# Re-timing one batch's input loads around a second-stage group, and two warm-up products, in a Fourier-mixing and feed-forward kernel

## The chip, the core and the metric

The kernel runs on one core of a Trainium2 chip. The metric is device time in microseconds (us) from the start to the end of one execution. Unless marked otherwise, times inside the kernel are counted in us from the first instruction of the profiled execution.

The engines have short names in the profile: PE is TensorE (matrix products, with PEld its weight loads), DVE is VectorE, ACT is ScalarE, POOL is GpSimd, and SP is SyncE, which here only issues transfers (DMAs).

## What is computed

```python
def _attn_ref(x):                       # x: (8, 3008, 256) float32
    X = np.fft.fft(x, axis=1)
    X = np.fft.fft(X, axis=2)
    return X.real.astype(np.float32)

def _moe_ref(x, w_in, w_out):           # x: (24064, 256), w_in: (256, 2048), w_out: (2048, 256)
    h = x @ w_in
    g = h * (1.0 / (1.0 + np.exp(-1.702 * h)))
    return (g @ w_out).astype(np.float32)
```

The output is `_moe_ref` of the first function's result, its eight batches laid end to end.

## The kernel before

**Work and steps.** The Fourier transform along the 3008 rows is split as 47 x 64. For each batch there is a first stage (`mix1`, products with the tables `w1`), a turn through a DRAM buffer (`spill` writes it, `fill` reads it back in three parts of 512 KB), a small rotation of one column (`rotate`), and a second stage (`stage2`, three groups of 64 small products). The transform along the 256 columns is folded into `w_in` at the start (`fold_w`), so that the feed-forward part reads the second stage's result directly. The main loop has 48 steps for a batch, 384 in all; a step takes one pair of 128-row blocks of the hidden layer for half of a second-stage group. In a step t, `begin` forms the hidden products, `forward` (line 649) is the activation on ACT, `sums` on POOL and DVE and `deeper` on DVE prepare operands of a fast matrix product, and `product` and `small_products` of step t - 3 and t - 4 form the output. Eight steps make a group, whose result is turned by DVE (line 793) and stored by four DMAs for each half; the halves go out near the end of the next eight steps (in batch 0, for instance, in steps 38 and 39, and 46 and 47).

**Work put between.** What belongs to the next batches is hung on steps with `at(t, fn, ...)` (line 987). A table `PLANS` (line 984) holds, for a batch b, the steps within it for: the 16 folds of batch b + 1 on POOL (`fold1`, lines 245 to 251, two parts for each of 8 chunks), the four first-stage groups of batch b + 1 (`mix1`), the first of the three fills (`filled`), the rotation, the four loads of batch b + 2 into the tile `xt` (`load_x`, line 212), and the three second-stage groups. Batch 0 has a row of its own, all others share the second row. A fold step can be negative: those folds of batch b + 1 then run in the last steps of batch b - 1.

So the x of batch 2 is loaded in steps of batch 0, and its first four folds run at steps 46 to 49: two at the end of batch 0, two at the start of batch 1. A fold reads all 111 partitions of `xt`, and so waits for all four loads. Each load is two DMAs, one from x and one from a mirrored copy `Xr`: 512 KB each for loads 0 and 2, 240 KB each for loads 1 and 3. The second-stage group of step 44 is that of batch 1's first block.

**Queues.** Nearly all DMAs are issued by SP, in program order: a DMA that waits holds all behind it. `paced(t)` (line 424) is a 4-byte DMA that reads a value that `forward(t)` writes; it holds SP's queue until that activation. Each fill, each load and each turn (`turn`, line 201, which makes `Xr`) has one ahead of it.

**Warm-ups.** `warm(n)` (line 359) does n products of 128 columns by 512 whose result nobody reads, each as two matmul instructions. In the start, before the main loop, two stand beside `fold_w(0)`: one before it and one (of the tile `small`) after it. `stage2(0, 0)` (line 979) follows, then DVE's transposes of its result (`turn_seconds`, line 400), which the first hidden products (`hidden`, tiles pa and pb) wait for.

Of the kernel before, what the change touches and what calls it, by code (L numbers as in the profile page):

```python
# [51 lines left out]
def free(ap, offset, *dims):  # L52
    return bass.AP(ap.tensor, ap.offset + offset, [list(ap.ap[0])] + [list(d) for d in dims])
# [68 lines left out]
def kernel(ctx: ExitStack, tc, x, w_in, w_out, tab1, tab2, out):  # L122
# [25 lines left out]
    small = const.tile([128, 4 * NB + 128 + 4 * H], F32, tag="small", name="small")  # L148
# [30 lines left out]
    def bank(name, tag=None):  # L179
        if tag is None:  # L180
            tag = spare.pop(0)
            spare.append(tag)
        if tag in ("o0", "o1"):
            return o_banks[int(tag[1])]
        if tag[0] == "l":
            return pot["low"][:, 512 * int(tag[1]):512 * int(tag[1]) + 512]
        return (rest if tag[0] == "o" else psp).tile([128, 512], F32, tag=tag, name=name)
# [171 lines left out]
    def warm(n, tag=None, of=wcs[0]):  # L359

        ps = bank("warm", tag)
        for _ in range(n):
            nc.tensor.matmul(ps[:], lhsT=of[:, 0:128], rhs=of[:, 0:512], start=True, stop=True)
# [11 lines left out]
    def rotate(b, a0=0, a1=NG, copy=None):  # L375

        col = t4t[b][:, a0:a1, H]
        ps = bank("psr")
        halves(ps[:, 0:a1 - a0], rot, col, start=True, stop=True)
        (copy or nc.vector.tensor_copy)(col, ps[:, 0:a1 - a0])  # L380

    def stage2(b, blk):

        pq, t4 = pqp.tile([128, 2, 512], F32, tag="pq", name="pq"), t4t[b]
        pqt[b, blk] = pq
        m = m2 if b else m2f
        ps = [bank("ps2") for _ in range(NU)]
        for cs in range(2):
            for h in range(2):
                for g in range(4):  # L390
                    for u in range(NU):
                        rows, at = slice(64 * u, 64 * u + 64), cs * 256 + h * 128
                        nc.tensor.matmul(ps[u][32 * g:32 * g + 32, at:at + 128], lhsT=m[rows, cs, h * RUN:(h + 1) * RUN],  # L393
                                         rhs=free(t4[rows, 4 * blk, cs * H + g // 2 + NB * (g % 2):], 0, [D, 4], [2, 32]),
                                         start=(cs == h == 0), stop=True, skip_group_check=True)
        turning.append((pq, ps, 1 if b or blk else 2))
# [3 lines left out]
    def turn_seconds():  # L400
        for pq, ps, parts in turning:
            for cs, u in [(cs, u) for cs in range(parts) for u in range(NU)]:
                nc.vector.transpose(free(pq[:], cs * 512 + u * RUN, [256, 4 // parts], [NU * RUN, 4], [1, RUN]),
                                    free(ps[u][:], cs * 256, [128, 4 // parts], [32, 4], [1, 32]))
        turning.clear()
# [29 lines left out]
    def load_out(n, eng):  # L435
        t = raw["out", n] = ring("raw").bitcast(U32).rearrange("p (n w) -> p n w", w=2)
        eng.dma_start(out=t[:].rearrange("p (f n) w -> p f (n w)", f=4),
                      in_=w_out[4 * n * 128:(4 * n + 4) * 128, :].bitcast(U32).rearrange("(p f) n -> p f n", p=128))
# [70 lines left out]
    def halved(n):  # L509

        s = summed[n] = pre["in", n][0]
        nc.vector.tensor_tensor(s[:, 0:512], wst[n][:, 0], wst[n][:, 1], op=ALU.add)
        nc.vector.tensor_tensor(s[:, 512:], wst[n][:, 0], wst[n][:, 1], op=ALU.subtract)
# [13 lines left out]
    def fold_w(n, tags=(None, None)):  # L527
        ps = [bank("psw", tag) for tag in tags]
        for cs in range(2):
            if n in summed:  # L530
                for odd_d in range(2):
                    c0 = NB * odd_d
                    nc.tensor.matmul(ps[cs][c0:c0 + NB], lhsT=cd[:, 0, cs, c0:c0 + NB], rhs=summed[n][:, 512 * odd_d:512 * odd_d + 512],  # L533
                                     start=True, stop=True, skip_group_check=True)
        for i in range(2 if n not in summed else 0):
            for cs in range(2):
                halves(ps[cs][:], cd[:, i, cs, :], wst[n][:, i, :], start=(i == 0), stop=(i == 1))
        for cs in range(2):

            nc.scalar.copy(wcs[cs][:, n * 512:(n + 1) * 512].rearrange("p (f c) -> p f c", f=4),  # L540
                           free(ps[cs][:], 0, [1, 4], [4, 128]))
# [428 lines left out]
    for h0 in (0, 512):  # L970
        high(in1, h0, 512)
        finish_in(1, h0, 512)
    load_out(1, nc.sync)
    warm(1, "o0")
    fold_w(0)
    warm(1, "o0", small)
    first_row(0)
    rotate(0, 0, 4, nc.scalar.copy)
    stage2(0, 0)
    turn_seconds()  # L980
    halved(1)

    extra = {}
    PLANS = (((*range(9, 18), 22, 23, 24, 25, 26, 29, 30), (20, 28, 28, 36), 37, 43, (39, 40, 41, 42), (8, 20, 44)),
             ([g + k for g in (0, 8, 16, 24) for k in range(-2, 2)], (4, 20, 28, 28), 31, 35, (36, 38, 40, 42), (4, 20, 36)))

    def at(t, fn, *args):
        extra.setdefault(t, []).append((fn, args))
# [21 lines left out]
    for b in range(B):  # L1010
        t0 = b * NBLK * NF
        if b + 2 < B:
            for k in range(3):
                at(t0 + 11 + k, paced, t0 + 11 + k)
                at(t0 + 11 + k, turn, b + 2, k)
        folds, groups, filled, turned_at, loads, seconds = PLANS[min(b, 1)]
        if b + 1 < B:
            for c in range(NCH):
                for part in range(2):
                    at(t0 + folds[2 * c + part], fold1, b + 1, c, part, nc.gpsimd)  # L1020
                if c % 2:
                    k = t0 + groups[c // 2]
                    at(k, mix1, b + 1, c // 2)
                    for half in range(2):
                            at(k + 1 + (k != 36) * (c // 2 % 2), spill, b + 1, half, c // 2)
            for blk in range(NBLK):
                at(t0 + filled + blk, paced, t0 + filled + blk)
                at(t0 + filled + blk, fill, b + 1, 4 * blk, 4 * blk + 4)
            if b + 2 < B:
                for k in range(4):  # L1030
                    at(t0 + loads[k], paced, t0 + loads[k])
                    at(t0 + loads[k], load_x, b + 2, k)
                at(t0 + 34, paced, t0 + 34)
                at(t0 + 34, load_ends, b + 2)
                at(t0 + 41, fold_ends, b + 2, nc.gpsimd)
            at(t0 + turned_at, rotate, b + 1, 0, NG, nc.scalar.copy)
        for blk in range(NBLK):
            nxt = (b, blk + 1) if blk + 1 < NBLK else (b + 1, 0)
            if nxt[0] < B:
                k = t0 + seconds[blk]  # L1040
                at(k, stage2, *nxt)
                at(k + 1, nyquist_out, *nxt)
                at(k + 1 + (nxt != (1, 0)), nyquist, *nxt)
# [125 lines left out]
```

## Time and profile before

| what | value |
|---|---|
| median of 3 runs | 1838.15 us (1837.58, 1838.15, 1840.1) |
| the profiled execution | 1839.32 us |
| its span, first to last instruction | 1837.5 us |
| mean granted TensorE clock | 0.998 |
| instructions | 55863 |
| DMA queue q1 (SP's) | 148270 packets, 99.09 MB |

One execution is profiled; its rows give durations and idle times of single instructions, its own time is 1.8 us longer than its span. A line of a group reads: line of the code, engine, operation, tile written <- tiles read, shape, count, then busy us and mean ns. A line of a timeline reads: start, duration, engine, line, operation, tiles, shape, count, and in brackets the engine's idle time just before and what ended it; "issue" there means that nothing which the profile shows was waited for. The share of a DMA stretch is the mean over the core's 16 DMA engines and can come out slightly over 1.

### The profile page before, as it was taken

What the parts mean: (1) busy time and instruction counts of PE and PEld (TensorE: products, weight loads), DVE (VectorE), ACT (ScalarE), POOL (GpSimd) and SP (SyncE); (2) the same over time, 40 slices, a digit from 0 to 9 for tenths busy, and PEclk for the clock granted to TensorE, in tenths of its full rate; (3) what the DMA queues carried; (4) which work ended last, traced back from release to release, by engine and by line L of the source; (5) the groups of instructions that cost most, each with busy time, mean ns of one, the idle gap of its engine ahead of it and who ended that gap; (6) DMA issues with size and microseconds to landing.
All of it is one profiled execution on the core that took longest, in us unless ns stands there. A gap on an engine that the chain in (4) does not pass through costs nothing.

```text
span 1837.5 us, 55863 instructions
## 1 busy us (share of the span) xinstructions
PE 1821.4 (99%) x23656; PEld 1400.3 (76%) x23656; DVE 1478.0 (80%) x1927; ACT 1138.0 (62%) x2238; POOL 992.7 (54%) x1070
## 2 busy tenths in 40 slices
PE   8999999999999999999999999999999999999998
PEld 4677777777777777877778777787777877777775
DVE  6988878887888778887888878888788887878774
ACT  4666656665666666666666666666666666656663
POOL 3785446654656546565456644576446653444442
PEclk9999999999999999999999999999999999999999
DMA  8811251113311151212402124021331012100011
GB/s 273 194 53 35 60 99 28 47 35 96 60 45 30 49 115 27 61 27 72 92 22 59 32 67 86 22 64 26 84 69 38 15 26 65 29 21 14 18 24 24
DMA packets 151687, 105.68 MB, mean 58 GB/s; under 512 B 106212, under 2 KB 133094, under 8 KB 150878
## 3 DMA queue, kind: packets, MB, share of 16 engines
q1 hardware_dynamic: 148270, 99.09, 22.3%
q8 instruction: 186, 3.05, 0.7%
q10 hardware_dynamic: 3168, 3.03, 0.6%
q14 instruction: 63, 0.52, 0.1%
HBM read 64.81 MB, written 48.05 MB: 61 GB/s over the span
## 4 chain that ended last, share of the span: by engine, by line
PE 96%; DMA 2%; DVE 1%; issue 0%; POOL 0%; ACT 0%; SPq 0%; DVEq 0%; POOLq 0%
PE x L196 35%; PE o L196 28%; PE low L740 26%; PE o L740 4%; PE low L273 1%; PE low L393 1%; DMA xt<-in_x_dram 1%; PE po L196 0%; DMA Td<-big 0%; DMA big<-in_moe_w_in_dram 0%; DMA Tf<-big 0%; DMA Td<-e 0%; PE psw L533 0%; PE ps L393 0%; POOL xt L905 0%
## 5 line engine op out<-in xcount | busy, mean ns | idle before, releaser
L664 POOL TENSOR_TENSOR big<-big 128x256 f32<-128x256 f32 (+1 forms) x376 | 365.7, 973 | 786.0 <-ACT big L656 772.0
L196 PE MATMUL x<-pq,wcs 128*64 128x256 f32 (+1 forms) x6016 | 765.0, 375 | 0.0
L196 PE MATMUL o<-big,wo 128*64 128x256 f32 (+1 forms) x4800 | 631.1, 376 | 0.0
L196 PEld LDWEIGHTS x<-pq,wcs 128*64 128x64 f32 x6016 | 422.8, 137 | 173.5 <-issue 1.5
L196 PEld LDWEIGHTS o<-big,wo 128*64 128x64 f32 x4800 | 337.7, 137 | 145.3 <-issue 8.2
L646 ACT ACTIVATE g<-x 128x512 f32<-128x512 f32 (+1 forms) x376 | 221.7, 590 | 362.3 <-PE x L196 359.9
L665 POOL TENSOR_TENSOR big<-big 128x256 f32<-128x256 f32 (+1 forms) x376 | 380.0, 1011 | 0.0
L740 PE MATMUL low<-big 128*64 128x128 f32 (+1 forms) x5888 | 377.5, 270 | 0.0
L649 ACT ACTIVATE big<-x 128x512 f32<-128x512 f32 (+1 forms) x376 | 221.7, 590 | 241.0 <-PE x L196 215.3
L634 ACT ACTIVATE x<-nb,af 128x256 f32<-128x256 f32 (+1 forms) x752 | 352.7, 469 | 12.2
L653 DVE TENSOR_TENSOR big<-g,x 128x512 f32<-128x512 f32 (+1 forms) x376 | 250.5, 666 | 132.2 <-ACT big L649 131.5
L740 PEld LDWEIGHTS low<-big 128*64 128x64 f32 x5888 | 335.1, 137 | 25.2
L695 DVE TENSOR_TENSOR big<-big 128x1024 f32<-128x1024 f32 (+1 forms) x184 | 225.4, 1225 | 101.4 <-PE low L740 85.8
L656 ACT ACTIVATE big<-big 128x512 f32<-128x512 f32 (+1 forms) x376 | 231.6, 616 | 24.5 <-DVE big L653 23.4
L740 PE MATMUL low<-big,wo 128*64 128x128 f32 (+1 forms) x2944 | 220.0, 270 | 0.0
L699 DVE TENSOR_TENSOR big<-big 128x512 f32<-128x512 f32 (+1 forms) x184 | 192.0, 1043 | 0.0
L697 DVE TENSOR_TENSOR big<-big 128x512 f32<-128x512 f32 (+1 forms) x184 | 168.1, 914 | 16.6 <-PE o L196 0.9
L740 PEld LDWEIGHTS low<-big,wo 128*64 128x64 f32 x2944 | 172.6, 137 | 6.3
L672 DVE TENSOR_TENSOR big<-big 128x512 f32<-128x512 f32 (+1 forms) x188 | 159.0, 845 | 6.5
L842 DVE TENSOR_TENSOR big<-big,low 128x512 f32<-128x512 f32 (+3 forms) x184 | 109.1, 610 | 35.6 <-PE low L740 32.2
L671 DVE TENSOR_TENSOR big<-big 128x512 f32<-128x512 f32 (+1 forms) x188 | 131.5, 700 | 0.9 <-POOL big L664 0.9
L740 PE MATMUL o<-big,wo 128*64 128x128 f32 (+1 forms) x1472 | 110.0, 270 | 0.0
(119 smaller groups left out, 1124.9 us busy)
## 6 DMA issues: line engine op xcount, KB each, us to landing
out_dram<-os SPq DMA_DIRECT2D x284, 64.0 KB
Td<-xt SPq DMA_DIRECT2D x56, 192.0 KB
t<-Td SPq DMA_DIRECT2D x21, 512.0 KB
xt<-in_x_dram SPq DMA_DIRECT2D x14, 512.0 KB
xt<-Xr SPq DMA_DIRECT2D x14, 512.0 KB
nb<-Nd SPq DMA_DIRECT2D x22, 256.0 KB
out_dram<-os SPq DMA_DIRECT2D x96, 56.0 KB
Xr<-in_x_dram SPq DMA_DIRECT2D x7, 752.0 KB
```

Of the source, the lines that this page charges most:

```text
L196: nc.tensor.matmul(out[c0:c0 + 64], lhsT=lhs[:, c0:c0 + 64], rhs=rhs, skip_group_check=True, **how)
L634: nc.scalar.activation(x[:, i * 256:i * 256 + n], nbt[b, blk][:, hh * 256:hh * 256 + n], ACTF.Copy, scale=af1[:, f:f + 1])
L646: nc.scalar.activation(two(g[:], n), two(xb[t][:], n), ACTF.Copy, scale=2.0)
L649: nc.scalar.activation(front(t), two(xb[t][:], width(t)), ACTF.Gelu_apprx_sigmoid)
L653: nc.vector.tensor_tensor(back(t), two(gt.pop(t)[:], n), two(xb.pop(t)[:], n), op=ALU.subtract)
L656: nc.scalar.activation(back(t), back(t), ACTF.Gelu_apprx_sigmoid)
L664: eng.tensor_tensor(right(t, S1, n), left(t, A21, n), right(t, A22, n), op=ALU.add)
L665: eng.tensor_tensor(left(t, S3, n), left(t, A11, n), left(t, A21, n), op=ALU.subtract)
L695: nc.vector.tensor_tensor(free(big[:], SUM, *both_), free(big[:], from11 + w, *twice), free(big[:], from11, [at_right(t, 0) + w - from11, ...
L697: nc.vector.tensor_tensor(s2, a11, s1, op=ALU.subtract)
L699: nc.vector.tensor_tensor(s4, a12, s2, op=ALU.subtract)
L740: nc.tensor.matmul(o, lhsT=lhs, rhs=rhs, start=first_in, stop=(p == NP - 2), skip_group_check=True)
```

## The change

Four things change in the schedule; no function does.

- In batch 0's plan the three fills of batch 1 move from steps 37, 38, 39 to 38, 39, 40, and the four loads of batch 2 from steps 39, 40, 41, 42 to 41, 42, 45, 46, that is two on each side of the second-stage group of step 44. Each moves with its pacing DMA.
- Batch 1 gets a plan row of its own, in which the first four folds of batch 2 run at steps 47 to 50 in place of 46 to 49. The other twelve stay, and so do the plans of batches 2 and later.
- Ahead of `fold_w(0)` there are two warm-up products in place of one.
- One more warm-up product, of `small`, stands between `stage2(0, 0)` and `turn_seconds()`.

```diff
     load_out(1, nc.sync)
-    warm(1, "o0")
+    warm(2, "o0")
     fold_w(0)
     warm(1, "o0", small)
     first_row(0)
     rotate(0, 0, 4, nc.scalar.copy)
     stage2(0, 0)
+    warm(1, "o0", small)
     turn_seconds()
     halved(1)
...
-    PLANS = (((*range(9, 18), 22, 23, 24, 25, 26, 29, 30), (20, 28, 28, 36), 37, 43, (39, 40, 41, 42), (8, 20, 44)),
+    PLANS = (((*range(9, 18), 22, 23, 24, 25, 26, 29, 30), (20, 28, 28, 36), 38, 43, (41, 42, 45, 46), (8, 20, 44)),
+             ([g + k for g in (1, 8, 16, 24) for k in range(-2, 2)], (4, 20, 28, 28), 31, 35, (36, 38, 40, 42), (4, 20, 36)),
              ([g + k for g in (0, 8, 16, 24) for k in range(-2, 2)], (4, 20, 28, 28), 31, 35, (36, 38, 40, 42), (4, 20, 36)))
...
-        folds, groups, filled, turned_at, loads, seconds = PLANS[min(b, 1)]
+        folds, groups, filled, turned_at, loads, seconds = PLANS[min(b, 2)]
```

## The prediction

> **What bounds the kernel now.** I read the page first, then PE's waits, then PE's timeline around each wait, then granted clock and busy time in short stretches, and at last SP's queue and the landings of its transfers.
>
> ```profile
> PE 1821.4 (99%) x23656; PEld 1400.3 (76%) x23656; DVE 1478.0 (80%) x1927; ACT 1138.0 (62%) x2238; POOL 992.7 (54%) x1070
> ...
> PE 96%; DMA 2%; DVE 1%; issue 0%; POOL 0%; ACT 0%; SPq 0%; DVEq 0%; POOLq 0%
> ```
>
> PE is the bound: 99% busy, 96% of the chain that ended last. The change takes no product away and adds two, so it can win only where PE stands still or runs slowly. After the start PE waits once for longer than 0.4 us:
>
> ```profile
> 247.08 1.03 PE L196 MATMUL x<-pq,wcs 128*64 128x256 f32 x8
> 248.04 0.94 PE L393 MATMUL low<-t,small 64*32 64x128 f32 x46
> 251.40 0.86 PE L393 MATMUL low<-t,small 64*32 64x128 f32 x18 [2.41 <-issue]
> 252.18 1.12 PE L196 MATMUL o<-big,wo 128*64 128x256 f32 x4
> 253.09 1.92 PE L196 MATMUL x<-pq,wcs 128*64 128x256 f32 x8
> ```
>
> This is stage2(1, 0) of step 44. It stops after 46 of its 64 products for 2.41 us, released by "issue", not by an operand, and the products behind it take 1.92 us where the same eight take 1.03. The stretches show both slow places; columns are the stretch, its length, busy us (instructions) of PE, PEld, DVE, ACT, POOL, then granted clock, DMA share and GB/s.
>
> ```profile
> 16.10:19.52 3.42, 2.37 (x42) 2.16 (x41) 2.73 (x5) 1.17 (x2) 0.00 (x0) 1.00 1.06 291
> ...
> 29.76:33.17 3.41, 2.04 (x84) 1.68 (x84) 3.21 (x6) 0.40 (x4) 1.81 (x2) 1.00 0.91 235
> 33.17:36.58 3.41, 3.01 (x14) 1.69 (x16) 2.17 (x6) 0.58 (x1) 0.77 (x1) 0.50 1.02 363
> ...
> 248.21:251.62 3.41, 1.00 (x62) 0.72 (x50) 2.17 (x4) 2.07 (x4) 1.80 (x2) 1.00 1.01 186
> 251.62:255.04 3.42, 3.42 (x32) 1.88 (x18) 1.89 (x3) 0.00 (x0) 0.06 (x1) 0.50 0.98 98
> ```
>
> The clock is 0.50 twice, each time for 3.41 us. The two falls lie 218.45 us apart, 64 times 3.413, and the first rise, at 5.86, lies 8 times 3.413 before the first fall: the clock is decided on a fixed grid. A grid stretch with PE busy for 2.04 us or 1.00 us was followed by half clock; one with 2.37 was not. I take the limit to lie between 2.04 and 2.37.
>
> **Price of the stall of step 44.** From the forward activation of step 44 (246.49) to that of 46 (262.12) are 15.63 us. Two plain steps are 4.78 + 4.32 = 9.10; a second-stage group adds 1.27 (batch 1: 4.29 + 6.08 around its group, less 9.10); the psn products add 0.87. That makes 11.24, so 4.39 us are lost: 2.41 standing still, 3.41/2 = 1.71 at half clock, 0.27 around them.
>
> **Why it stalls.** Transfer queue q8 carries instructions: 186 packets for 47,785 PE records, one per 257. In the packet records the n-th starts, when nothing is in its way, as PE passes record 158 + 256n. Packet 21 was due so at 239.93 and started at 248.39, 8.46 us late; it took 1.37, and PE went on at 251.40, 1.64 after its end. PE ran dry at 248.98. Packet 22 was 7.9 late while PE stood still; of the rest the latest (5.49) still left 2.1 us by the same count. What stood before it is in SP's queue:
>
> ```profile
> 234.47 0.63 SPq L218 DMA_DIRECT2D xt<-Xr  x1
> 235.18 0.40 SPq L425 DMA_DIRECT2D Tk<-big  x1
> 235.63 0.35 SPq L218 DMA_DIRECT2D xt<-in_x_dram  x1
> 236.03 0.92 SPq L218 DMA_DIRECT2D xt<-Xr  x1
> 237.01 0.40 SPq L425 DMA_DIRECT2D Tk<-big  x1
> 237.46 0.34 SPq L218 DMA_DIRECT2D xt<-in_x_dram  x1
> 237.91 0.60 SPq L218 DMA_DIRECT2D xt<-Xr  x1
> ```
>
> Landing medians are 239.5 and 242.6 (load 0), 244.9 and 247.1 (load 1), 249.6 and 252.6 (load 2), 255.1 and 257.1 (load 3). The packet started 1.2 before the first landing of load 2, so it had waited out all issued before that. Batches 1 and 2 agree: packet 42 was due at 439.97, behind two transfers issued at 438.53 and 438.95, and started at 444.49, 1.2 before the second landed (445.65); packet 65 started 0.6 before (667.19, 667.78). Rule from the rows: a packet starts 0.6 to 1.2 us before the landing of the last transfer issued ahead of it.
>
> The Trainium skill (DMA: Bandwidth & Descriptors, Queues, rings and completion order) says that each DMA engine takes turns between queues after each packet of some 9 to 17 descriptors. By that the fetch waits for one share of a transfer; the 8.46 us speak against it.
>
> **The change, part by part.** Times are those of before.
>
> *Fills at 38 to 40, from 37 to 39.* The one at 217.30 goes; the next two places (226.51, 232.66) stay, and the third takes the place of load 0 (234.04). It puts one more 512 KB fill ahead of the loads: 1.45 us, from the three of batch 1 that land 1.48 and 1.45 apart. It lands at 236.85 + 1.45 = 238.3; rotate needs it at 245.24. Cost there nothing.
>
> *Loads at 41, 42, then 45, 46.* Load 0 follows at once (its pacing value is there from 233.54), issued near 234.8. Load 1 waits for step 42's activation, which ends at 237.87, so its halves are issued near 238.2 and from 238.6 to 239.5: just before packet 21 is due (239.7; the eight instructions of two more warm-ups bring it forward 0.2). Load 1 thus still stands ahead of it, load 2 no longer. Load 0 lands at 238.3 + 2.6 = 240.9 and 2.4 to 3.1 later, load 1 at 2.3 and 2.15 more: 247.8 to 248.5. The packet starts at 246.7 to 247.9, I take 247.4, needs 1.0 on an emptying queue, and PE goes on 1.64 later, near 250.05. Against 248.98 the stall is 1.05 us (0.4 to 1.9), not zero. The stretch then has about 3.41 - 1.05 = 2.36 busy, the upper edge of the limit, so I take the clock to stay. Loss 1.05 in place of 4.39: **gain 3.3** (0.8 to 4.4).
>
> *What loads 2 and 3 meet.* Load 2 waits for step 45's activation (255.71) with only step 46's stores behind it on SP; packet 23 (due 260.57) then waits to about 262 and has until 272. Load 3 goes behind the four stores of step 46 (266.02 to 267.9): issued near 268.3 and 268.65, landing near 272.9 and 275.3 (4.2 and 6.0 after the start in batch 1, and the stores ahead). On POOL the first fold of batch 2, now at step 47, is reached at 271.9 and waits 3.4 us; behind it the sums of steps 48 to 50 come 2.8, 1.9 and 1.0 late. DVE reads the sums of 49 at 281.57; POOL would have them at 275.3 + 1.5 + 1.9 + 1.9 + 1.0 = 281.6. The fourth fold ends at 287.9 and the first-stage group needs it at 290.98. Cost nothing, with no slack at DVE and 1.6 us behind it, where the o banks are emptied (285.4) before PE's products (287.0).
>
> *Warm-ups.* One is 0.95 us (three took 2.84). The first fills the pause before fold_w (psw starts at 24.70, the one before streams until 23.76). The second follows stage2(0, 0), which streams until about 32.4, and ends near 33.4, while pa waits for DVE's transposes until 33.57. Together 0.1, bounds 0 and 1.9 if both pauses were gone. The second puts 0.6 to 0.7 us into the stretch 29.76 to 33.17: 2.04 becomes 2.65, above the limit. The half clock after it goes: pa and pb need 0.87 each again, **gain 1.7** (0 to 1.7). DVE waits for pb at 37.10 (1.76 us), so its chain moves too; w_out block 1 lands at 44.84 and is read at 46.65, so it bears 1.7 earlier.
>
> The Trainium skill (TensorE: Matmul & The Clock Gate, Why this matters for your kernels) asks only for gaps under about 3 us to keep the clock. By that no warm-up would be worth anything here; yet half clock followed a stretch whose longest gap is 0.83 us.
>
> **Sum.** The profiled execution took 1839.32 us (span 1837.5, 1.8 around it), 1.2 above the median of 1838.15; the three runs spread over 2.5 us, more than one half-clock stretch is worth, and my sum is absolute for a run without them: 1839.32 - 3.3 - 1.7 + 0.1 = **1834.4**.
>
> **Rivals.**
> - *The stall goes altogether:* packet 21 comes before load 1's second half. Then it starts near 245 and PE never runs dry: gain 4.4, 1833.3. For: the second half is issued only 0.2 to 1.1 us before it is due. Against: packet 65, due 0.5 us after such an issue began, still waited for it. By the turn-taking rule above it would also come out so. Chance 0.25.
> - *The clock still falls after the stall:* 1.4 us or more stand still in one stretch. 1834.4 + 1.7 = 1836.1, up to 1837. Chance 0.22.
> - *The first half clock stays:* the warm-up counts for less than its busy time, or another position of the grid finds the thin stretch 29.6 to 31.5. 1836.1. Chance 0.13.
> - *Slower:* load 3 lands late and POOL, held by the fold, becomes the bound. PE pays from a landing at 277 on, one for one. In this burst load 2's second half needed 14.7 us from issue to landing; load 3 with that lands at 283.3, 6.3 past the point: 1840.7. Against: the DMA share is near nothing from 258 to 266. Chance 0.05.
> - *Forecast:* 0.35.
>
> The range takes in all but the last and the worst of the clock cases: 1832.8 to 1837.3. About 0.2% (3.7 us, below 1834.5) is what a measurement of this kernel can tell from no change: the forecast sits on that line. Faster: 0.25 and somewhat over half of 0.35, so 0.46; same 0.49; slower 0.05.
>
> **What would show it.** In the changed kernel's trace: the half-clock stretch at 33 gone and pa of hidden(0) at 1.03 us; packet 21 starting 1 us earlier against PE's records, PE's wait in stage2(1, 0) near 1 us; the forward activations of 44 to 46 some 12.3 us apart; POOL waiting for a load before L245 at step 47 with no wait of PE behind it. I am wrong if that wait is over 1.9 us or zero, if the clock falls anywhere after 6 us, or if PE waits near step 50 to 52.

## The result, and the profile after

The changed kernel takes 1834.5 us (median of 15 runs, 1832.91 to 1837.45), the kernel before 1838.45 beside it (15 runs, 1835.88 to 1843.06). The ratio is 0.9977, 95% interval 0.9969 to 0.9985: by the ratio 4.2 us less, with 2.8 to 5.7 inside the interval. The profiled execution took 1834.38 us (span 1832.6), 4.94 less than that of before.

The page of the changed kernel, PE's row and the chain:

```profile
PE 1820.0 (99%) x23660; PEld 1398.6 (76%) x23660; DVE 1480.1 (81%) x1927; ACT 1138.4 (62%) x2238; POOL 993.6 (54%) x1070
...
PE 97%; DMA 2%; DVE 1%; POOL 0%; issue 0%; ACT 0%; SPq 0%; DVEq 0%; POOLq 0%; ACTq 0%
```

PE is the bound as before, with 4 instructions more and 1.4 us less busy time; in the chain "issue", which stood fourth, now stands fifth. PE's timeline around stage2(1, 0) of step 44:

```profile
246.74 1.03 PE L196 MATMUL x<-pq,wcs 128*64 128x256 f32 x8
247.70 1.20 PE L393 MATMUL low<-t,small 64*32 64x128 f32 x64
248.83 0.65 PE L196 MATMUL o<-big,wo 128*64 128x256 f32 x4
249.31 1.03 PE L196 MATMUL x<-pq,wcs 128*64 128x256 f32 x8
```

All 64 products stand in one row without a bracket: no wait. The eight products behind them take 1.03 us, so the clock is full. The forward activations of 44 and 46 start at 246.14 and 257.38, 11.24 us apart, exactly the sum of the plain parts; before they lay 15.64 apart (the prediction has 15.63, by rounding). The whole 4.40 us are back.

SP's queue at the loads, and the stretches of the start (columns as in the prediction):

```profile
233.91 0.33 SPq L218 DMA_DIRECT2D xt<-in_x_dram  x1
234.34 0.62 SPq L218 DMA_DIRECT2D xt<-Xr  x1
237.55 0.23 SPq L425 DMA_DIRECT2D Tk<-big  x1
237.82 0.35 SPq L218 DMA_DIRECT2D xt<-in_x_dram  x1
238.22 0.91 SPq L218 DMA_DIRECT2D xt<-Xr  x1
```

```profile
29.95:33.36 3.41, 3.41 (x89) 1.88 (x86) 3.22 (x4) 1.48 (x5) 1.99 (x3) 1.00 0.86 207
33.36:36.78 3.42, 3.42 (x40) 1.64 (x22) 3.01 (x8) 0.58 (x1) 1.27 (x1) 1.00 1.02 388
```

Instruction packet 21 is due at 239.36 (PE's record 158 + 256 x 21, as in the prediction) and starts at 243.87 by the packet records, 4.51 late in place of 8.46, although both halves of load 1 were issued before it was due. The start shows no half clock. But the start gave only 0.35 us in these two executions: the forward activation of step 8 comes at 81.35, before at 81.70. From there to that of step 44 are 164.8 us in both, then 4.40 are won, and from step 46 to the last forward another 0.14.

### The profile page after: what moved, and what is told of

It reads as the page before. It is cut to its first block, busy times and chain, and to the rows that moved or that the text cites. A ratio compares the mean times of both kernels' runs of the same rounds, so it can differ in the third digit from the quotient of the medians.

```text
span 1832.6 us, 55868 instructions
## 1 busy us (share of the span) xinstructions
PE 1820.0 (99%) x23660; PEld 1398.6 (76%) x23660; DVE 1480.1 (81%) x1927; ACT 1138.4 (62%) x2238; POOL 993.6 (54%) x1070
## 4 chain that ended last, share of the span: by engine, by line
PE 97%; DMA 2%; DVE 1%; POOL 0%; issue 0%; ACT 0%; SPq 0%; DVEq 0%; POOLq 0%; ACTq 0%
PE x L196 35%; PE o L196 28%; PE low L740 26%; PE o L740 4%; PE low L273 1%; PE low L393 1%; DMA xt<-in_x_dram 1%; PE po L196 0%; DMA Td<-big 0%; DMA big<-in_moe_w_in_dram 0%; DMA Td<-e 0%; DMA Tf<-big 0%; PE psw L533 0%; POOL xt L905 0%; PE ps L393 0%
```

## The experiments

Ratios are to the kernel before, timed beside each kernel. "Distance" is that between the forward activations of steps 44 and 46 in the profiled execution (11.24 without loss). "Lead" is the time from the start of the issue of load 1's first half to the moment when packet 21 is due (negative: issued after it), "late" is how late the packet starts.

| kernel | median us | ratio, 95% interval | lead | late | distance |
|---|---|---|---|---|---|
| before | 1838.45 | 1 | 4.29 | 8.46 | 15.64 |
| changed | 1834.5 | 0.9977, 0.9969 to 0.9985 | 1.54 | 4.51 | 11.24 |
| e1 warm-ups only | 1837.66 | 0.9996, 0.9988 to 1.0005 | 5.24 | 8.51 | 15.50 |
| e2 plans only | 1835.18 | 0.9986, 0.9978 to 0.9995 | 1.76 | 7.45 | 13.06 |
| e3 folds back | 1839.37 | 1.0006, 0.9998 to 1.0015 | 1.53 | 4.49 | 11.22 |
| e4 load 1 at 41 | 1835.0 | 0.9976, 0.9968 to 0.9985 | 0.53 | 5.39 | 11.25 |
| e5 plans only, load 1 at 43 | 1835.74 | 0.9977, 0.9968 to 0.9986 | -3.01 | 1.93 | 11.25 |
| e6 two early warm-ups fewer | 1836.33, one run | none | 1.76 | 7.58 | 12.87 |
| e7 only loads 2 and 3 moved | 1834.35 | 0.9976, 0.9967 to 0.9985 | 4.16 | 6.73 | 12.01 |
| e8 load 1 at 43 | 1834.12 | 0.9973, 0.9961 to 0.9984 | -3.23 | 2.31 | 11.25 |
| e9 no warm-ups in the pauses | 1836.0 | 0.9982, 0.9974 to 0.9991 | -2.79 | 2.70 | 11.25 |
| e10 more warm-ups | 1835.5 | 0.9979, 0.9970 to 0.9988 | -3.56 | 2.46 | 11.25 |

**e1: the kernel before, with both added warm-ups.**

```diff
-    warm(1, "o0")
+    warm(2, "o0")
...
     stage2(0, 0)
+    warm(1, "o0", small)
```

> Before with the two warm-up products alone. Theory (two separate gains): the half clock near 33 us goes, the stall of step 44 stays. Forward activations of steps 44 and 46 lie 15.6 us apart as before, packet 21 is about 8.5 us late and PE waits 2.4 us in stage2(1, 0). From the first fold_w product's place in line (the warm-up ahead of fold_w) to the first add of rows(0) it takes about 12.3 us, as in the changed kernel, against 14.3 before. Time 1.5 to 2.0 us under before. Rival (the start is bound by its loads, whatever PE does): the half clock goes and the time moves by under 0.5 us.

The stall stayed (2.22 us idle on "issue", and half clock from 252.84), and the start of the profiled execution had no half clock. The time is 0.7 us under that of before by the ratio (0.9 above to 2.2 below), which settles neither the theory (1.5 to 2.0) nor the rival (under 0.5): the warm-ups alone are not what the change brought. The profile can't show their gain either: the forward activation of step 8 comes at 81.98 here, at 81.70 before, and over the twelve profiles anywhere from 79.80 (e2) to 84.50 (e7).

**e2: the changed kernel without the added warm-ups.**

```diff
-    warm(2, "o0")
+    warm(1, "o0")
...
-    warm(1, "o0", small)
     turn_seconds()
```

> The changed kernel without both added warm-ups: fills, loads and folds moved, nothing else. Theory: stall of step 44 gone (44 to 46 in 11.2 us, no PE wait in stage2(1, 0)), half clock near 33 us as before or not by the position of the grid; time 3.9 to 4.6 us under before. Rival (the profile of before caught an unusually long stall, and the unprofiled runs mostly have a smaller one): the trace shows the stall gone all the same, but the time falls by 2 to 3 us only.

PE's timeline of e2 at step 44:

```profile
246.15 0.94 PE L393 MATMUL low<-t,small 64*32 64x128 f32 x46
248.55 0.61 PE L393 MATMUL low<-t,small 64*32 64x128 f32 x18 [1.46 <-issue]
249.10 0.65 PE L196 MATMUL o<-big,wo 128*64 128x256 f32 x4
249.58 1.03 PE L196 MATMUL x<-pq,wcs 128*64 128x256 f32 x8
```

The expectation, no stall, failed. This is the stall that I had forecast for the changed kernel: behind the same 46 products, inside the forecast's 0.4 to 1.9 us, at full clock behind it. It is there without the warm-ups of the start, 200 us earlier, and gone with them. Two explanations were open: the warm-ups' eight PE instructions bring packet 21 forward against the steps, or their work in the pauses matters by itself.

**e6: both pauses filled as in the changed kernel, eight instructions fewer at the head of the program.**

```diff
-    warm(6)
+    warm(4)
```

> The changed kernel with four warm-ups fewer... that is, the first call at the head of the program makes 4 instead of 6 warm-up groups, so that PE's record of every later product comes 8 earlier while both pauses are filled as in the changed kernel. Theory (the position in PE's instruction stream decides): packet 21 is due about 0.3 us later against the steps, as in the run with the plan alone; load 1's first half, issued 1.4 us or more before, is ahead again, PE waits about 1.5 us in stage2(1, 0) and the forward activations of 44 and 46 lie 13.06 us apart. Rival (the work in the pauses itself, or the time at which the start ends): no wait, 11.24 us.

PE's timeline of e6 at step 44:

```profile
247.95 0.95 PE L393 MATMUL low<-t,small 64*32 64x128 f32 x46
250.16 0.62 PE L393 MATMUL low<-t,small 64*32 64x128 f32 x18 [1.26 <-issue]
```

The stall is back, behind the same 46 products, and the distance is 12.87 (1.63 lost). So the position in PE's instruction stream decides. Packet 21 is due 6.56 us ahead of step 44's forward here (239.82, 246.38) and 6.78 ahead of it in the changed kernel (239.36, 246.14): the lead of load 1 goes from 1.76 to 1.54 with it, and the packet's lateness from 7.58 to 4.51. It is one profile of each, and e6 has no other run, but e2 (1.76, 7.45) and e3 (1.53, 4.49) stand beside them.

**e4: load 1 at step 41.**

```diff
-    (41, 42, 45, 46)
+    (41, 41, 45, 46)
```

> The changed kernel with load 1 at step 41 in place of 42, right behind load 0: issued near 235 to 236.5, 3 us before packet 21 is due, not 1. Queue theory (an instruction packet waits for all transfers that were issued some 1 to 2 us or more ahead of it): packet 21 starts 0.6 to 1.2 us before load 1's second half lands, near 246.5, about 7 us late; PE goes on near 249.1 and stands still for 0.2 to 1.2 us in stage2(1, 0); 0.3 to 1.3 us over the changed kernel, more if the clock falls. Turn theory (the DMA engine takes the instruction packet after the transfer it has in hand): packet 21 starts near 243.9 as in the changed kernel, no wait of PE, time the same.

This did not test what it was to test. The second pacing DMA of step 41 writes the cell that the first one writes, waited for it to land (239.26), and load 1 went out later than in the changed kernel, not earlier. What is left is one more row of the table: a lead of 0.53, no wait.

**e7: load 1 well ahead of the packet, by the old steps of fills, load 0 and load 1.**

```diff
-    38, 43, (41, 42, 45, 46)
+    37, 43, (39, 40, 45, 46)
```

> The changed kernel with the fills back at steps 37 to 39 and loads 0 and 1 at steps 39 and 40, as before the change; only loads 2 and 3 stay at 45 and 46. Theory (a packet waits for all that was issued well ahead of it): load 1 is issued some 3 to 4 us before packet 21 is due and wholly ahead, the packet starts as load 1's second half lands, near 245.5 to 247, and PE waits 0.7 to 2 us; the forward activations of 44 and 46 lie 12 to 13.1 us apart, 1835.3 to 1836.3. Rival (each queue takes turns with the instruction queue, and only the number of transfers in flight counts): no wait, 11.24 us, 1834.5.

```profile
250.83 0.91 PE L393 MATMUL low<-t,small 64*32 64x128 f32 x42
252.14 0.65 PE L393 MATMUL low<-t,small 64*32 64x128 f32 x22 [0.39 <-issue]
```

The stall is there and smaller than expected: 0.39 us idle where 0.7 to 2 were forecast, distance 12.01, 0.77 lost. Loads 2 and 3 were most of the old wait; the turn-taking rival (no stall) falls. The median (1834.35, forecast 1835.3 to 1836.3) does not resolve the 0.77.

**e5 and e8: load 1 behind the packet, without and with the added warm-ups.**

```diff
-    (41, 42, 45, 46)
+    (41, 43, 45, 46)
```

> The changed kernel without its two added warm-ups, and with load 1 of the first batch at step 43 instead of 42. Theory: what counts is which transfers are issued well before instruction packet 21 is due; without the warm-ups and with load 1 at step 42 (the run with the plan alone) load 1's first half was ahead, PE waited 1.46 us and the forward activations of 44 and 46 lay 13.06 us apart. With load 1 at step 43 it is issued after the packet is due, so the packet waits for load 0 alone, starts near 243, PE doesn't wait and the distance is 11.2 us: 1.8 us less than the plan alone, 1833.4. Rival, that the warm-ups' work in the pauses is what took the wait away: the wait of about 1.5 us stays, 13.0 us, 1835.2.

> The changed kernel with load 1 at step 43 instead of 42. Theory: packet 21 waits for load 0 alone in the changed kernel already, so its start (243.9) and PE's 11.24 us between the forward activations of 44 and 46 stay, and the time too, 1834.5, while the packet has load 1 no longer anywhere near it. Rival (load 1, 0.2 to 1.1 us before the packet, still delays it in part): the packet starts 0.5 to 2 us earlier; the time is the same, since PE waits in neither.

PE does not wait in either, and the packet starts only 1.93 and 2.31 late: load 1 did delay it by some 2.2 us in the changed kernel too, but not into a wait, so e8's theory fell and its rival (0.5 to 2 us) came near. The distance of e5 is the forecast one, its time is not (1835.74 for 1833.4): four of its ten runs had two half-clock stretches or more, as counted below. By the ratios e5 lies 1.7 us under e2 (0.9977, 0.9986), about what moving load 1 by a step wins in the distance, 1.80, but the intervals overlap, so the times do not show it. e8 is the lowest median of the study (1834.12); its interval does not separate it from the changed kernel. By an estimate its packet could start 3.7 us later still before PE lost time (6.0, worked out below, less 2.31), that of the changed kernel 1.5, or 1.0 with the 1.86 us that its packet took.

**e3: the changed kernel with the first four folds of batch 2 at steps 46 to 49, as before.**

```diff
-([g + k for g in (1, 8, 16, 24) for k in range(-2, 2)], (4, 20, 28, 28), 31, 35, (36, 38, 40, 42), (4, 20, 36)),
+([g + k for g in (0, 8, 16, 24) for k in range(-2, 2)], (4, 20, 28, 28), 31, 35, (36, 38, 40, 42), (4, 20, 36)),
```

> The changed kernel with batch 2's first four folds back at steps 46 to 49. POOL reaches the first fold at about 261.9 and waits for load 3 until 270.4: 8.4 us in place of 3.3. Behind it the sums of steps 47, 48 and 49 come about 6.0, 3.4 and 2.5 us late. Theory (POOL's slack is spent): DVE's sums and the fast products of steps 47 and 48 wait, PE loses 1 to 4 us near steps 49 to 51; time 1 to 4 us over the changed kernel. Rival (POOL has slack enough, the fold's move was not needed): PE has no wait near these steps and the time is that of the changed kernel within 0.5 us.

POOL's, DVE's and PE's timelines of e3, one row of each:

```profile
271.94 0.21 POOL L245 TENSOR_TENSOR xt<-xt 111x4 f32<-111x4 f32 x1 [8.44 <-issue]
```

```profile
274.21 1.87 DVE L671 TENSOR_TENSOR big<-big 128x512 f32<-128x512 f32 x1 [4.80 <-POOL big L664]
```

```profile
276.14 0.65 PE L196 MATMUL o<-big,wo 128*64 128x256 f32 x4 [2.96 <-DVE big L671]
```

Read downwards this is one wait handed on: the fold waits 8.44 us for load 3, POOL's sums behind it come late, DVE waits 4.80 for them and PE 2.96 for DVE. From the forward activation of step 49 to that of step 50 are 7.61 us, in the changed kernel 4.33: 3.28 lost. The kernel is no faster than before (1.0006): with the folds a step earlier, all of the gain is lost. By the ratios that is 5.3 us, more than this one wait; 8 of the 12 runs list a mean clock of 0.998 or less, none of the changed kernel's, and where in them the clock fell is known for the profiled run alone (at 32.44, in the start). The changed kernel's own row is the other side of it, POOL waiting 3.26 us and nobody behind it:

```profile
270.48 0.21 POOL L245 TENSOR_TENSOR xt<-xt 111x4 f32<-111x4 f32 x1 [3.26 <-issue]
```

**e9 and e10: the pauses of the start, on the base of e8.** e9 takes away all three calls of `warm` there, e10 has more.

```diff
-    warm(2, "o0")
     fold_w(0)
-    warm(1, "o0", small)
...
     stage2(0, 0)
-    warm(1, "o0", small)
```

```diff
-    warm(2, "o0")
+    warm(4, "o0")
...
     stage2(0, 0)
-    warm(1, "o0", small)
+    warm(2, "o0", small)
```

> The changed kernel with load 1 of the first batch at step 43, and without any of the four warm-ups around fold_w(0) and stage2(0, 0), the two old ones and the two added ones. Packet 21 comes due about 0.6 us later against the steps, but load 1 is issued 3 us or more after that in any case, so PE doesn't wait in stage2(1, 0) and the forward activations of 44 and 46 lie 11.2 us apart. Theory (the pauses of the start make the clock fall, and the warm-ups in them hold it): a half-clock stretch falls before 40 us in most runs; each that falls lowers the mean clock of a run by 0.0009 and costs 1.4 us, so the median is 1835.5 to 1837, 1 to 3 us above the same kernel with its warm-ups (1834.1). Rival (the start varies by itself, and the warm-ups do nothing for the clock): 1834.1, clocks of 0.999 as there.

> The changed kernel with load 1 of the first batch at step 43 and twice the added work in the pauses: four warm-ups ahead of fold_w(0) in place of two, two behind stage2(0, 0) in place of one. Theory (the warm-ups hold the clock in the pauses, and the changed kernel's are enough in most runs): no half clock before the end in nearly any run; what runs past the pauses costs 0 to 2 us: 1834.1 to 1836. Rival (the warm-ups do nothing for the clock): clocks as with fewer of them, and the same 0 to 2 us. Rival (the pauses still let the clock fall in the changed kernel now and then, and more warm-ups would help): 1833 to 1833.8. No wait of PE in stage2(1, 0), 11.2 us.

Both times came out inside their forecasts. Each run lists its mean granted clock. A half-clock stretch takes 0.5 x 3.41 / 1835 = 0.0009 from it. Every profile here also ends at half clock, for 0.9 us (e1) to 3.9 us (e4), which takes up to 0.0011. So a run that lists 1.0 had no other stretch, one at 0.998 or less had at least one, one at 0.997 at least two, and 0.999 leaves it open: the profiled execution of e5 lists 0.999 with a stretch from 34.76, that of the changed kernel 0.999 without one. Least counts, then, among kernels without a wait of PE at step 44 or near step 50:

| kernel | warm-up products in the pauses | runs at 0.998 or less |
|---|---|---|
| e9 | 0 | 9 of 11 |
| e5 | 2 | 4 of 10 |
| changed, e4, e8 | 4 | 0 of 15, 0 of 11, 0 of 6 |
| e10 | 7 | 0 of 11 |

The falls become rarer as the warm-ups come. Seven of e9's nine and all four of e5's list 0.997; with four warm-ups none of 32 runs lists 0.998 or less, 12 of them list 1.0 and 20 leave it open. Four are not always enough: of the seven profiles with them (changed, e1, e3, e4, e6, e7, e8) two show a fall in the start. In e7 the clock fell at 28.59, where PE stood still before fold_w(0) until 28.70, and 2 of 10 runs list 0.998; in e3 it fell at 32.44. e10's extra ones run past the pauses (stage2(0, 0) to DVE's first normalization, line 614: 5.09 us against 4.24) and cost about 1 us. The stretches of e9:

```profile
22.99:26.41 3.42, 1.57 (x29) 1.33 (x25) 3.14 (x5) 2.80 (x5) 2.21 (x3) 1.00 0.82 247
26.41:29.82 3.41, 3.29 (x16) 0.97 (x16) 1.28 (x2) 1.22 (x2) 1.74 (x3) 1.00 0.73 274
29.82:33.23 3.41, 2.19 (x77) 1.54 (x80) 3.13 (x4) 1.45 (x5) 2.08 (x3) 1.00 0.71 166
33.23:36.65 3.42, 2.58 (x41) 1.36 (x27) 3.00 (x7) 0.00 (x0) 1.26 (x1) 0.50 0.98 382
```

The clock fell behind a stretch with 2.19 us of work and held behind one with 1.57.

## Why the prediction was right, and where it was not

The time came out as forecast, 1834.4 against 1834.5, and that it came so near is luck: two steps were off in opposite directions. The stall gave 4.4 us in the profiles where I had 3.3, and the clock of the start 0.7 by e1, with a wide interval, where I had 1.7. Of my own signs of error one came true here: PE's wait in stage2(1, 0) is zero.

**The bound, the price of the stall and its cause: right.** The distance went from 15.64 to 11.24, the plain parts to the hundredth. That the wait is one for instructions is shown by e6, which changes nothing near step 44 and has it back. The price can be read from the packet: PE ran dry 9.05 us after the packet was due, the packet takes 1.37 and PE goes on 1.64 after it, so lateness beyond 9.05 - 1.37 - 1.64 = 6.0 us is lost. That gives 2.4 (before), 1.5 (e6), 1.4 (e2) and 0.7 (e7); the distances lost 2.7 (4.40 less the half clock's 1.71), 1.63, 1.82 and 0.77.

**"Load 1 thus still stands ahead of it": the step that failed.** The places were right: packet 21 due at 239.7 (239.71 when shifted to before's steps by 0.35), load 1 landing as forecast (its second half at 247.95 for 247.8 to 248.5). The rule that whatever is issued before the packet is due stands ahead of it was not. Leads of 1.54 us and less left the packet 4.5 to 5.4 late (changed, e3, e4), leads of 1.76 made it 7.6 and 7.5 late (e6, e2), and with load 1 behind it, it was 1.9 to 2.7 late (e5, e8, e9, e10). So at step 44 load 1 held the packet back fully only when its issue began 1.76 us ahead, not 1.54. The changed kernel's lead is 1.54; I had 0.2 to 1.5 in view and called it ahead. The term came to 4.4 where I had 3.3: the first rival, for this part.

No single limit fits all rows. In before itself the second half of load 2 was issued 2.02 us before packet 21 was due, in e1 2.85 us, and neither was waited out: the packet started 4.2 and 3.6 us before they landed (medians 252.57 and 252.04). So the rule did not even hold in the burst from which I had read it. Packet 65, by which I had argued against the rival, switches just as sharply, but elsewhere: it starts 5.4 to 5.5 us late where the first half of its load was issued 0.90 us or more ahead (before, e2, e5, e6, e9), 2.6 to 2.9 late in the changed kernel, e3, e4, e7 and e10 (0.78 to 0.88), and 4.7 and 4.9 late in e8 and e1 (0.88, 0.89). What sets the limit stays open.

The Trainium skill (DMA: Bandwidth & Descriptors, Queues, rings and completion order) has each DMA engine change queues after a packet of some 9 to 17 descriptors. The stall went, as by that rule, but the packets do not fit it: their lateness grows from 2.3 (e8) to 4.5 (changed) to 8.5 us (before) with the transfers issued ahead, and e7 still stalls. The Trainium skill (Runtime: NRT & Kernel Launch, Instruction fetch mechanics) says that PE's instructions come in blocks of 256 and that crossing a block is mostly hidden. The trace agrees with the block (186 packets, one per 257 records) and with "mostly": one crossing in 186 was not. PE ran dry 291 records after the packet was due in all five kernels that stalled (before, e1, e2, e6, e7).

**"The half clock after it goes: gain 1.7": probably too large, because one profile stood for all runs.** In the profile of before it fell, and a stretch of it costs 1.4 us, read off the start: from stage2(0, 0) to line 614 are 5.6 us with it (before, e3, e5) and 4.14 to 4.25 without (changed, e1, e2, e4, e6, e7, e8). But with the warm-ups that before has, it does not fall in each run, and not always for one stretch. Of e5's ten runs three list 1.0, so no stretch, four list 0.997, so two or more, and the profiled one had one: at least 9 stretches in 10 runs, 0.9 x 1.4 = 1.3 us by this estimate. e1 measures 0.7, with an interval from -0.9 to 2.2, which does not exclude 1.7. The mechanism was right: from e9 (at least 9 of 11 runs) to e10 (none seen in 11) the falls go as the warm-ups come. A fall after 6 us I had named as a sign of error; the changed kernel's only one, at 1828.77, lies past the last forward (1814.45), as one of before at 1835.40 does (1819.33).

**The limit of busy time, "between 2.04 and 2.37": fell.** e9 above, and e2, where the stretch from 246.72 had 1.95 us of work and the clock stayed, while it fell in e7 behind one with 1.05. The third way in which PE could have lost 1.7 us, the fall behind a stall, thus wasn't decided by the sum I made. The Trainium skill (TensorE: Matmul & The Clock Gate, Why this matters for your kernels) asks only that there be no gap over about 3 us. In e9 the longest gap before the fall is 1.94 us, and the clock fell in at least 9 of 11 runs; the measurement decides against the rule here. Neither the longest gap nor the busy time of a stretch told which would fall.

**Fills, loads 2 and 3, folds: right.** Shifted to the times of before (by 4.74, the difference at step 46), load 3 was issued at 268.25 and 268.64 (forecast 268.3, 268.65) and landed at 272.6 and 274.6 (272.9, 275.3). POOL waited 3.26 for a forecast 3.4, and the steps from 48 to 52 last as before. That there was no slack at DVE could be tested only one step to the other side: e3 pays 3.28 us there.

**The sum.** By the profiles: 0.35 + 4.40 + 0.14 and 0.05 around them make the 4.94. By the runs: 0.7 for the warm-ups (e1), and from e1 to the changed kernel 0.9996 - 0.9977, 3.5 us, for the rest. That is less than 4.40, which fits that the half clock behind the stall does not fall in each run either: 4 of e1's 11 runs, which all carry that schedule, list a clock of 1.0. My sum started from 1839.32, an execution 0.9 above the median of before with both half clocks in it; with the measured terms, 3.5 + 0.7 from 1838.45 gives 1834.2, which closes the account and tests nothing.

## What to carry to other kernels

Where PE waits on "issue" with every operand there, look for the instruction queue's packet that came late, and at which transfers were issued in the microseconds before it was due; spread that burst, so that the next large transfer is issued well after the packet is due (2.8 to 3.6 us after, in the four runs with the least delay). Such a wait depends on the count of instructions ahead of it: eight fewer at the head of the program brought it back in e6, so a small edit far away can do so, and the version with distance to it (e8) is the one to keep, though its time is not told apart. And a stretch seen once in one profile is a chance, not a term: count it over the runs, here by the mean clock that each one lists, as far as that tells, before it goes into a sum.

## What the runs showed of the hardware that was not expected

- Whether a transfer delays an instruction packet hangs on a fraction of a microsecond: load 1 issued 1.54 us or less before packet 21 was due made it some 2 us later than with load 1 behind it, issued 1.76 us before some 5 (4.5 to 5.4 and 7.5 to 7.6 us late, against 1.9 to 2.7). At packet 65 the switch lies near 0.9 us.
- PE can run dry on a single packet of 186: packet 21 is asked for 291 instruction records ahead, 9.1 to 9.3 us at this kernel's pace in steps 43 and 44.
- The clock's fall is a matter of chance from run to run in the same kernel (at least 5 of 10 in e5, 9 of 11 in e9), on a grid whose start differs between executions (first rises at 5.86, 6.05, 7.45 and 8.11 us in four profiles), and little work in a stretch does not foretell it (held behind 1.57 us, fell behind 2.19).
- A pacing DMA of 4 bytes needed 4.7 us from issue to landing with load 0 issued right behind it (e4), and the next one, which writes the same cell, was held until then.
